# Attention beside projections: score tiles in groups of three steps up to step 236

## The chip, the cores and the metric

The kernel runs on one core of a Trainium2 chip. The core has a matrix engine (TensorE; PE in the profile, with PEld for its weight loads), a vector engine (VectorE, DVE), an activation engine (ScalarE, ACT), GpSimd (POOL) and a queue engine (SyncE, SP) that issues transfers. What is measured is the device time of one execution in microseconds (us); less is better. The time before is the median of three runs.

## The reference

The program is a stack of four sublayers on a sequence of 2048 rows with 640 columns: attention, Fourier mixing, attention, Fourier mixing, all with the same weights. Each works on a layer norm of its input and is added to it.

```python
def _A_ref(x, wqkv, wo):            # H = 32 heads, Dh = 20
    qkv = (x @ wqkv).reshape(B, S, 3, H, Dh) ...
    scores = jnp.einsum("bhqd,bhkd->bhqk", q, k) * (Dh ** -0.5)
    p = _softmax(scores, axis=-1)
    o = jnp.einsum("bhqk,bhkd->bhqd", p, v)
    return o.transpose(0, 2, 1, 3).reshape(B, S, D) @ wo
...
x = x + _A_ref(_layernorm(x), A_wqkv, A_wo)
x = x + _B_ref(_layernorm(x), ...)  # Real(DFT_seq(DFT_hidden(x)))
x = x + _A_ref(_layernorm(x), A_wqkv, A_wo)
x = x + _B_ref(_layernorm(x), ...)
```

Everything is computed in 32-bit floats. Projections are made as three products of split operands (high times high, high times low, low times high), so that they are exact enough.

## The kernel before

A layer has a prologue (layer norm, transposes, the first chunks of q and k, half of v), the attention, the output projection and the Fourier part. The change is in the attention.

**Steps.** Attention is a list of 512 steps in each layer (`Attention.steps`): eight groups `g` of four heads, four blocks `qb` of 512 queries, sixteen blocks `kc` of 128 keys. `scores(n, j)` makes one score tile of step n, for two heads: two matmuls of 62 rows, side by side in the array (rows 0 and 64), into one of three PSUM banks that go round, `p{(2n+j)%3}`, and then one exponential on ScalarE over 128 x 1024 elements into one of seven buffers `e`, which go round as well. A step has two score tiles. `values(n)` multiplies the four exponentials of a step with v and adds into one PSUM bank, `acc`; each of its four matmuls shows as two records in the profile. After the last key block, `finish` transposes that bank out on VectorE, normalizes, and stores on GpSimd's queue. In the profile the score matmuls are `psc`, the values `acc`, the exponentials `e<-psc`.

**Blocks.** The rest of q, k and v is projected during the attention. `Qkv.work()` gives it out in blocks of matmuls into one PSUM bank (`fill`): a product of 15 matmuls (five chunks, three passes) is cut by `pieces` into eight and seven, for a q or k chunk of 128 columns (`pqk`, 512 wide) and for v (`pv`, 320 wide). A q or k product is then split on VectorE and stored (`keep`), and two steps later a small matmul makes the norms of it (`pn`, `norms`). A v product is only copied out (`own`). `need` asks that a chunk be made before a group of heads begins to load it, and gives out blocks at once if it isn't.

**Sweep.** `sweep` sets the order by hand. For each step it calls `begin` (tasks, bounds, needs), issues the loads of q and k on SyncE's queue, makes the two score tiles, calls `fill` (which gives out at most one block, if `due` says that blocks are behind their marks), and then some values. Up to step `THIN` = 236, a step with a block makes no values (unless kc is 1), and the next step makes all that are owed, up to two steps behind the scores. After step 236 blocks are sparser and values follow under another rule, which stays. The marks before are 16 blocks by step 44 and 74 by step 236; 107 are all.

**Loads.** `qload` fetches the next block of q, with a bound for the exponent (`shiftb`), at kc 4 of the block before. For the groups in `LATE` (4 and 6 before) it goes at kc 10, with a bound made anew in each block (`bound`: kc 5, 8 and 10), so that their q chunk need be made only a block of 512 rows at a time.

**Other work.** `compare` gives VectorE a few tasks of a check that runs along (the tiles `cq`, `far`, `ctop`); ScalarE does hardly anything but exponentials in the attention.

Of the kernel before, what the change touches and what calls it, by code (L numbers as in the profile page):

```python
# [23 lines left out]
GUARD = 30.0  # L24
NP = NT // 2
NQ = NT // 4
LATE = (256 // (4 * DH) + 1, 512 // (4 * DH))
FIRST = (0, 1, 4, 5)
HD = D // 2
TOL = 2.0 ** -32  # L30
# [5 lines left out]
def mha_fnet_kernel(ctx, tc, x_in, wqk, wv, wo, seq, hid, nat_seq, nat_hid, out):  # L36
# [65 lines left out]
    def pieces(blocks, n):  # L102

        todo = [f for b in blocks for f in b]
        for i in range(0, len(todo), n):
            for f in todo[i:i + n]:
                f()
            yield i + n < len(todo)
# [23 lines left out]
    class Qkv:  # L132
# [248 lines left out]
        def work(s):  # L381

            order = [ND + 1, 1, ND + 2, 2, ND + 3, 3, ND + 4, 4]
            w = {0: s.w1}

            def chunk(i):
                c = order[i]
                for tb in range(NB):
                    p = bank("fill", [128, 512], "pqk")
                    for more in pieces([s.product(p, w[i], tb, dc) for dc in range(ND)], 8 if (i, tb) < (5, 1) else 5):  # L390
                        if more:
                            yield True
                    sq = s.keep(p, c, tb, True, s.fill)

                    def after():
                        s.norms(bank("fill", [H, 512], "pn"), c, tb, sq)
                        s.made.add((c, tb))
                        if tb == NB - 1:
                            s.made.add(c)
                            if i + 1 < len(order):  # L400
                                w[i + 1] = s.weights(s.fill("w", [2, ND, 128], F32R, "wqk"), order[i + 1], True)
                            if i + 2 < len(order):
                                s.fetch(order[i + 2])
                    yield after

            for i in range(4):
                yield from chunk(i)
            for t in range(NT):
                p = bank("fill", [128, HD], "pv")
                for more in pieces([s.value(p, t, dc) for dc in range(ND)], 8):  # L410
                    if more:
                        yield True
                s.own(p, t, 1, True)
                yield None
            s.made.add("v")
            for i in range(4, 8):
                yield from chunk(i)

            s.silent = True
            r = s.bounds()  # L420
            ok = const.tile([128, 1], F32, name="ok", bufs=2)
            V.tensor_scalar(ok[:H], r[:H, 2:3], (GUARD / SCALE) ** 2, None, op0=OP.is_le)

            def after():
                p = bank("fill", [1, 1], "pok")
                PE.matmul(p, ok[:H], one[:H], start=True, stop=True)
                V.tensor_scalar(s.flag, p, float(H), None, op0=OP.is_equal)
            yield after
# [25 lines left out]
    class Attention:  # L454
# [95 lines left out]
                    G.dma_start(s.o[k, h * DH:(h + 1) * DH, qb * 512:(qb + 1) * 512],  # L550
                                hl[k][32 * j:32 * j + DH])

        def sweep(s, shift, begin, fill):
            done = calm = 0
            for n, (g, qb, kc) in enumerate(s.steps):
                begin(n, g, qb, kc)
                last = qb == NB - 1
                if kc == (7 if last else 10 if g in LATE else 4) and not (last and g == H // 4 - 1):
                    s.qload(*((g, qb + 1) if not last else (g + 1, 0)), shift)
                if last and g + 1 < H // 4:  # L560
                    for f, j in {1: [(0, 0)], 9: [(0, 1)], 11: [(1, 0)]}.get(kc, []):
                        s.kload(g + 1, f, j)
                if qb == 0 and kc == 0 and g:
                    s.kload(g, 1, 1)
                s.scores(n, 0)
                s.scores(n, 1)

                more, owed = fill(n) and n >= 2 and n + 1 < len(s.steps), n - 1 - done  # L570
                if n < s.THIN:
                    if more and kc != 1:
                        continue
                    count = owed
                else:
                    if more and owed < 3:
                        calm = n + 2
                        continue
                    count = min(owed, 1)
                    if owed > 1 and (done + 1) % NT and n >= calm:  # L580
                        calm = n + 2
                        count = 2
                for _ in range(count):
                    s.values(done)
                    done += 1
            for n in range(done, len(s.steps)):
                s.values(n)

        def run(s, done, project, check):

            work, tasks, later = s.a.work(), s.a.vweights(1, s.a.fill, pause=[lambda: None] * 2), list(check)
            s.work, s.blocks, s.after, s.rest, s.more, s.landed = True, 0, None, 0, False, 0

            marks = ((0, 0), (44, 16), (s.THIN, 74))

            def due(n):
                for (n0, k0), (n1, k1) in zip(marks, marks[1:]):
                    if n < n1:
                        return s.blocks < k0 + (k1 - k0) * (n - n0) / (n1 - n0)
                return s.blocks < 74 or s.blocks >= 107 or (n - 1) % NT in (2, 7, 12)  # L600

            def block(n):
                try:
                    f = next(work)
                    s.blocks += 1
                    s.more = f is True
                    s.after = (n + (2 if n < s.THIN else 4), f) if f and not s.more else None
                    s.rest = s.after[0] + 2 if s.after else n
                except StopIteration:
                    s.work = False  # L610
                    tasks.extend(done())

            def fill(n):
                if s.after:
                    if n >= s.after[0]:
                        f, s.after = s.after[1], None
                        f()
                elif s.work and n >= s.rest and (s.more and n < s.THIN or due(n + 1)):
                    block(n)
                    s.rest = max(s.rest, n + 2)  # L620
                    return s.work and not s.a.silent

            def compare(n):


                if n < 8:
                    return
                for _ in range(2):
                    if not later or n < s.landed or (len(check) - len(later)) * 490 >= n * len(check):
                        break  # L630
                    task = later.pop(0)
                    if isinstance(task, tuple):
                        s.landed = n + 5
                        task = task[1]
                    task()

            def need(n, *keys):
                while not all(k in s.a.made for k in keys):
                    if s.after:
                        fill(s.after[0])  # L640
                    else:
                        block(n)

            def begin(n, g, qb, kc):


                if qb == NB - 1 and g + 1 < H // 4:
                    when, to = 0, g + 1
                    c0, c1 = to * 80 // 128, ((to + 1) * 80 - 1) // 128
                    keys = [c0, (c1, 0) if to in LATE else c1, ND + c0, ND + c1] + (["v"] if to >= 4 else [])  # L650
                else:
                    when, to, keys = 5, g, [(((g + 1) * 80 - 1) // 128, qb + 1)]
                if to != g or g in LATE and qb < NB - 1:
                    if kc == when:
                        need(n, *keys)
                        s.shift = s.a.bound(to, s.room)
                    if kc - when in (0, 3, 5):
                        next(s.shift)

                if tasks and n % 2 == 0 and n >= 16 and n % 64 < 54:  # L660
                    tasks.pop(0)()
                for f in project.early.get(n, []):
                    f()

            def between(n):
                more = fill(n)
                compare(n)
                return more

            s.sweep("b", begin, between)  # L670
            assert not s.work and not later and not tasks, (len(later), len(tasks))

        def general(s, done, project):
# [35 lines left out]
                for j in range(2):  # L709
                    s.kload(0, f_, j)  # L710
            s.qload(0, 0, "m")
            s.sweep("m", lambda *_: None, lambda *_: None)
            for f in sum(project.early.values(), []):
                f()

# [813 lines left out]
```

## Time and profile before

| | |
|---|---|
| median of the runs | 2512.77 us (2511.39 to 2512.98) |
| profiled execution | 2511.93 us, its span 2510.1 us |
| busy: PE / ACT / DVE / POOL | 2479.9 / 2133.1 / 980.2 / 524.1 us |
| score matmuls (L518) | 4096, 786.2 us |
| value matmul records (L529) | 8192, 1057.9 us |
| exponentials (L521) | 2048, 1934.4 us |
| attention, layer 0, first score to step 236 | 86.6 to 598.5 us |
| attention, layer 1, first score to step 236 | 1330.2 to 1842.4 us |

The profile is of one execution. Its time includes some 2 us outside of the span. A matmul's end is modelled, so busy time of PE is no measure of how much it could still do; what counts is the time from the start of one run of equal matmuls to the start of the next. A row of the timeline merges equal instructions that follow each other: start, length, engine, line, operation, tiles written and read, shapes, and how many (x). In brackets stands how long the engine had been idle and what released it.

### The profile page before, as it was taken

The numbers are of one execution on the slowest core, as the hardware profiler recorded it, in microseconds if no ns is written. First come the engines' busy times: TensorE is split into PE (matmuls) and PEld (weight loads), VectorE is DVE, ScalarE is ACT, GpSimd is POOL, SyncE is SP. The second block draws the span as 40 slices with busy tenths as digits, with TensorE's granted clock in tenths as the row PEclk, the third lists the DMA queues.
The fourth block names the chain that finished last, engine by engine and source line by source line (L and its number), as shares of the span: only waits on it lengthen the run. The fifth ranks groups of instructions, "written<-read, shape, count | busy, mean of one in ns | idle before, by whom it ended". The sixth has DMA issues, their size and how long they took to land. (4 is left out here: it accounts for less than half of the span.)

```text
span 2510.1 us, 43669 instructions
## 1 busy us (share of the span) xinstructions
PE 2479.9 (99%) x16350; PEld 1147.5 (46%) x16350; DVE 980.2 (39%) x2144; ACT 2133.1 (85%) x2430; POOL 524.1 (21%) x1028
## 2 busy tenths in 40 slices
PE   8999999999999999999999999999999999999998
PEld 7644434433333332249885444444433333322596
DVE  6245422234243333416753444223233333332275
ACT  6688899989999999985457888999899999999752
POOL 2012111111212212113321121111121122221233
PEclk9999999999999999999999999999999999999999
DMA  5224221223222224327553332212131322233355
GB/s 188 95 88 126 81 90 44 83 72 94 86 90 86 94 86 123 118 89 245 190 182 100 114 111 91 80 57 65 59 100 51 92 62 71 58 108 96 115 211 195
DMA packets 127241, 262.58 MB, mean 105 GB/s; under 512 B 28952, under 2 KB 53304, under 8 KB 127020
## 3 DMA queue, kind: packets, MB, share of 16 engines
q1 hardware_dynamic: 88428, 159.83, 19.7%
q0 software_dynamic: 38592, 99.85, 12.6%
q8 instruction: 132, 2.16, 0.4%
q14 instruction: 89, 0.73, 0.1%
HBM read 175.29 MB, written 84.26 MB: 103 GB/s over the span
## 5 line engine op out<-in xcount | busy, mean ns | idle before, releaser
L521 ACT ACTIVATE e<-psc 128x1024 f32<-128x1024 f32 x2048 | 1934.4, 1121 | 126.0 <-PE psc L518 94.1
L529 PE MATMUL acc<-e,v 128*32 128x512 f32 x8192 | 1057.9, 602 | 3.9 <-DVE of L536 3.8
L518 PE MATMUL psc<-stq,stk 62*128 62x512 f32 x4096 | 786.2, 455 | 1.3 <-ACT e L521 1.3
L518 PEld LDWEIGHTS psc<-stq,stk 62*128 62x128 f32 x4096 | 335.5, 184 | 792.3 <-ACT e L521 762.6
L529 PEld LDWEIGHTS acc<-e,v 128*32 128x32 f32 x8192 | 188.9, 108 | 381.6 <-issue 358.4
L99 PE MATMUL pqk<-xt,wqk 128*128 128x512 f32 x1200 | 319.6, 407 | 2.1 <-DVE top L213 1.4
L550 POOL DMA_DIRECT2D o<-oh x256 | 131.5, 522 | 872.5 <-DVE oh L545 871.4
L84 DVE CAST hl<-pqk 128x512 fp32r<-128x512 f32 x64 | 44.3, 692 | 553.5 <-PE pqk L99 553.5
L99 PEld LDWEIGHTS pqk<-xt,wqk 128*128 128x128 f32 x1200 | 213.2, 188 | 90.3 <-issue 43.5
L536 DVE STREAM_TRANSPOSE of<-acc 128x512 f32<-128x512 f32 x64 | 45.8, 716 | 349.9 <-PE acc L529 349.3
L99 PE MATMUL pv<-wv,xt 128*128 128x320 f32 x960 | 159.7, 316 | 0.0
L99 PEld LDWEIGHTS pv<-wv,xt 128*128 128x128 f32 x960 | 141.1, 188 | 24.7 <-issue 21.2
L550 POOL DMA_DIRECT2D o<-ot x256 | 128.5, 510 | 1.9 <-issue 1.4
L207 POOL DMA_DIRECT2D scrq<-hl x40 | 28.1, 704 | 446.1 <-DVE hl L87 311.4
L243 DVE COPY v<-pv 128x320 f32<-128x320 f32 x32 | 15.7, 491 | 235.3 <-PE pv L99 235.3
L765 DVE TENSOR_REDUCE far<-cq 128x1 f32<-128x512 f32 (+5 forms) x169 | 98.5, 584 | 5.7
L92 PE MATMUL py<-wo,o 128*128 128x320 f32 x320 | 99.1, 310 | 1.4 <-DVE xr L947 1.4
L207 POOL DMA_DIRECT2D scrk<-hl x40 | 28.0, 699 | 344.3 <-DVE hl L87 300.2
L93 PE MATMUL py<-wo,o 128*128 128x320 f32 x320 | 98.6, 308 | 0.0
L94 PE MATMUL py<-wo,o 128*128 128x320 f32 x320 | 98.6, 308 | 0.0
L769 DVE TENSOR_TENSOR cq<-cq 128x512 f32<-128x512 f32 (+4 forms) x166 | 96.4, 580 | 2.4 <-DMA cq<-in_nat_seq_dram 2.4
L213 DVE TENSOR_REDUCE top<-pn 32x1 f32<-32x512 f32 x80 | 53.5, 676 | 107.4 <-PE pn L212 107.4
(200 smaller groups left out, 1729.2 us busy)
## 6 DMA issues: line engine op xcount, KB each, us to landing
cq<-in_nat_seq_dram POOLq DMA_DIRECT2D x64, 512.0 KB, 5.3
scrq<-hl POOLq DMA_DIRECT2D x40, 512.0 KB, 3.2
scrk<-hl POOLq DMA_DIRECT2D x40, 512.0 KB, 3.2
stq<-scrq SPq DMA_DIRECT2D x256, 80.0 KB
stk<-scrk SPq DMA_DIRECT2D x128, 160.0 KB
o<-o SPq DMA_DIRECT2D x16, 1280.0 KB
stq<-scrq SPq DMA_DIRECT2D x256, 40.0 KB
stk<-scrk SPq DMA_DIRECT2D x128, 80.0 KB
```

The source lines that it names most:

```text
L92: PE.matmul(out_ap, ah, bh, start=start, stop=False)
L93: PE.matmul(out_ap, ah, bl, start=False, stop=False)
L94: PE.matmul(out_ap, al, bh, start=False, stop=stop)
L99: yield lambda i=i, j=j, k=k: PE.matmul(out_ap, a[i], b[j], start=dc == 0 and k == 0, stop=dc == ND - 1 and k == 2)
L207: G.dma_start(s.scr["qk"[k]][c * 128:(c + 1) * 128, :, tb * 512:(tb + 1) * 512], hl.bitcast(F32))
L213: V.tensor_reduce(s.top[:H, c // ND, c % ND, tb:tb + 1], p, op=OP.max, axis=AX.X)
L518: PE.matmul(p[:, i], s.k[g, kc // 8, j][r, kc % 8 * 128:(kc % 8 + 1) * 128], s.q[g, qb, j][r], start=True, stop=True)
L521: A.activation(e, p, AF.Exp, scale=SCALE)
L529: PE.matmul(s.acc[32 * j:32 * j + 32], s.a.v[kc][:, v0:v0 + 32], s.e[n, j // 2][:, j % 2], start=kc == 0, stop=kc == NT - 1, skip_group_ch ...
L550: G.dma_start(s.o[k, h * DH:(h + 1) * DH, qb * 512:(qb + 1) * 512], hl[k][32 * j:32 * j + DH])
L765: V.tensor_reduce(to, x, op=OP.max, axis=AX.X, apply_absolute_value=True)
L769: V.tensor_tensor(y, x, y, op=op)
```

## The change

Up to step 236, where a block is due (`plan`), three steps are now taken together: three score tiles, the block, three score tiles, and then the values of three steps, from the one before the group on. Groups begin at key blocks 1 to 14 only. A step outside of a group makes its two score tiles and all values that are owed, now up to one step behind. Blocks up to step 236 come only in groups. A v product is no longer cut (a piece of 15), so 91 blocks are all, and the mark is 58 blocks by step 236, at an even pace from the start. Group 1 joins `LATE`: its q chunk (the second) need be made only block by block. The tasks on VectorE (`compare`) follow the scores instead of the block. The rest of the diff passes these functions into `sweep` and counts n one later, without effect on the order after step 236.

```diff
-LATE = (256 // (4 * DH) + 1, 512 // (4 * DH))
+LATE = (1, 4, 6)
...
-                for more in pieces([s.value(p, t, dc) for dc in range(ND)], 8):
+                for more in pieces([s.value(p, t, dc) for dc in range(ND)], 15):
...
-        def sweep(s, shift, begin, fill):
-            done = calm = 0
-            for n, (g, qb, kc) in enumerate(s.steps):
+        def sweep(s, shift, begin, fill=lambda n: None, plan=None, compare=lambda n: None):
+            done = calm = n = 0
+
+            def opened(n):
+                g, qb, kc = s.steps[n]
                 begin(n, g, qb, kc)
...
+            while n < len(s.steps):
+                opened(n)
+                piece = plan and plan(n)
+                if piece:
+
+                    for t in range(2 * n, 2 * n + 6):
+                        if t > 2 * n and t % 2 == 0:
+                            opened(t // 2)
+                        s.scores(*divmod(t, 2))
+                        if t == 2 * n + 2:
+                            piece()
+                        if t % 2:
+                            compare(t // 2)
+                    n += 3
+                    while done < n - 1:
+                        s.values(done)
+                        done += 1
+                    continue
                 s.scores(n, 0)
                 s.scores(n, 1)
                 more, owed = fill(n) and n >= 2 and n + 1 < len(s.steps), n - 1 - done
-                if n < s.THIN:
-                    if more and kc != 1:
-                        continue
-                    count = owed
+                compare(n)
+                n += 1
+                if plan and n <= s.THIN:
+                    count = owed + 1
+                elif more and owed < 3:
+                    calm = n + 1
+                    continue
                 else:
-                    if more and owed < 3:
-                        calm = n + 2
-                        continue
...
-            marks = ((0, 0), (44, 16), (s.THIN, 74))
+            marks = ((0, 0), (s.THIN, 58))
...
-                return s.blocks < 74 or s.blocks >= 107 or (n - 1) % NT in (2, 7, 12)
+                return s.blocks < 58 or s.blocks >= 91 or (n - 1) % NT in (2, 7, 12)
...
-                elif s.work and n >= s.rest and (s.more and n < s.THIN or due(n + 1)):
+                elif s.work and n >= max(s.rest, s.THIN) and due(n + 1):
...
+            def plan(n):
+                if n % NT in range(1, NT - 1) and n + 3 <= s.THIN and not s.after and n >= s.rest and (s.more or due(n + 1)):
+                    return lambda: block(n + 1)
...
-            s.sweep("b", begin, between)
+            s.sweep("b", begin, fill, plan, compare)
```

More of the change, by code (lines that the diff above doesn't have):

```diff
@@ L570, in sweep @@
                 more, owed = fill(n) and n >= 2 and n + 1 < len(s.steps), n - 1 - done
-                if n < s.THIN:
-                    if more and kc != 1:
-                        continue
-                    count = owed
-                else:
-                    if more and owed < 3:
-                        calm = n + 2
-                        continue
+                compare(n)
[5 more added lines that the diff above has]
+                    continue
+                else:
                     count = min(owed, 1)
-                    if owed > 1 and (done + 1) % NT and n >= calm:
-                        calm = n + 2
+                    if owed > 1 and (done + 1) % NT and n > calm:
+                        calm = n + 1
                         count = 2
@@ L663, in begin @@
                     f()
[L665 to L668, printed above, removed]
-            s.sweep("b", begin, between)
+            s.sweep("b", begin, fill, plan, compare)
             assert not s.work and not later and not tasks, (len(later), len(tasks))
@@ L711, in general @@
             s.qload(0, 0, "m")
-            s.sweep("m", lambda *_: None, lambda *_: None)
+            s.sweep("m", lambda *_: None)
             for f in sum(project.early.values(), []):
```

## The prediction

> **What bounds the kernel now.** I read the busy time by stage first, then TensorE's timeline inside one stage, then ScalarE's. In each layer I cut the attention at the first score matmul of step 236, which is found by counting four score matmuls per step.
>
> ```profile
> 86.60:598.50 511.90, 508.82 (x3395) 210.34 (x3394) 185.94 (x376) 453.52 (x473) 89.56 (x158) 1.00 0.28 87
> 598.50:1118.40 519.90, 519.68 (x3511) 172.42 (x3507) 181.52 (x397) 514.01 (x554) 99.35 (x179) 1.00 0.30 92
> 1330.20:1842.40 512.20, 508.56 (x3395) 210.22 (x3394) 183.12 (x360) 453.80 (x473) 89.37 (x159) 1.00 0.28 86
> ```
>
> Columns: stretch, length, then busy time of PE, weight loads, DVE, ACT, POOL, and the clock (1.00). After step 236 ACT is busy 514.0 of 519.9 us with its exponentials, whose number stays, so nothing here can move that stretch. Up to step 236 (511.9 us in layer 0, 512.2 in layer 1) ACT has 58 us to spare and PE is full. The change lives there, twice. One unit of projection work in that stretch looks like this on PE:
>
> ```profile
> 210.36 2.14 PE L99 MATMUL pqk<-xt,wqk 128*128 128x512 f32 x8
> 212.43 0.73 PE L518 MATMUL psc<-stq,stk 62*128 62x512 f32 x4
> 213.09 1.92 PE L529 MATMUL acc<-e,v 128*32 128x512 f32 x16
> 214.94 0.73 PE L518 MATMUL psc<-stq,stk 62*128 62x512 f32 x4
> 215.61 1.91 PE L99 MATMUL pqk<-xt,wqk 128*128 128x512 f32 x7
> 217.44 0.73 PE L518 MATMUL psc<-stq,stk 62*128 62x512 f32 x4
> 218.10 1.92 PE L529 MATMUL acc<-e,v 128*32 128x512 f32 x16
> 219.96 0.73 PE L518 MATMUL psc<-stq,stk 62*128 62x512 f32 x4
> 220.63 1.24 PE L529 MATMUL acc<-e,v 128*32 128x512 f32 x8
> 221.80 0.73 PE L518 MATMUL psc<-stq,stk 62*128 62x512 f32 x4
> 222.46 1.07 PE L529 MATMUL acc<-e,v 128*32 128x512 f32 x8
> 223.46 0.73 PE L518 MATMUL psc<-stq,stk 62*128 62x512 f32 x4
> 224.12 0.50 PE L99 MATMUL pqk<-xt,wqk 128*128 128x512 f32 x1
> ```
>
> Durations are modelled, so I price a run from its start to the next run's start. Scores of a step: 0.66. Values of one step (8 records): 1.00; of two (16): 1.85, so a step more is 0.86 and each run of values has a fixed 0.14. Projection pieces: 2.07 for eight matmuls, 1.83 for seven, 0.24 per matmul. A lone step is 221.80 to 223.46, 1.66; one with the norms matmul (pn) is 1.84 (219.96 to 221.80). ACT has gaps here, so PE's switches cost time.
>
> **The change on PE alone.** Three score tiles in a row need one price that the steady part lacks. It stands at the start of layer 0, where PE (and PEld, its weight loads) shows:
>
> ```profile
> 89.35 0.98 PE L518 MATMUL psc<-stq,stk 62*128 62x512 f32 x6
> 89.93 0.40 PE L518 MATMUL psc<-stq,stk 62*128 62x512 f32 x2
> 90.97 0.19 PEld L518 LDWEIGHTS psc<-stq,stk 62*128 62x128 f32 x2 [1.09 <-ACT e L521]
> 90.97 0.50 PE L518 MATMUL psc<-stq,stk 62*128 62x512 f32 x2 [0.65 <-ACT e L521]
> 91.40 0.50 PE L99 MATMUL pqk<-xt,wqk 128*128 128x512 f32 x1
> ```
>
> The x6 row is 0.98 long where an x4 row is 0.73, so a third pair costs about 0.24: three tiles take 0.90, and the third starts 0.58 after the first (89.35 to 89.93). A pair that had to wait (90.97) takes 0.43 until the next run; an unhindered last pair takes 0.90 - 0.58 = 0.32. A wait in mid-run costs 0.11 on top, its weight load not having been made before.
>
> A projection unit now takes 6 steps; in the new order of the instructions it takes 8: group with eight matmuls, group with seven, a lone step with pn, a lone step.
> - Before, 8 steps: 224.12 - 210.36 = 13.76, plus two lone steps 3.32: 17.08.
> - After: (0.90 + 2.07 + 0.90 + 2.71) + (0.90 + 1.83 + 0.90 + 2.71) + 1.84 + 1.66 = 16.42, with three steps of values at 1.85 + 0.86 = 2.71.
> - Saved: 0.66, the two runs of scores and two of values that are gone.
>
> A unit of v (320 columns):
>
> ```profile
> 320.44 0.87 PE L518 MATMUL psc<-stq,stk 62*128 62x512 f32 x4
> 321.23 1.43 PE L99 MATMUL pv<-wv,xt 128*128 128x320 f32 x8
> 322.60 0.73 PE L518 MATMUL psc<-stq,stk 62*128 62x512 f32 x4
> 323.26 1.92 PE L529 MATMUL acc<-e,v 128*32 128x512 f32 x16
> 325.12 0.73 PE L518 MATMUL psc<-stq,stk 62*128 62x512 f32 x4
> 325.78 1.29 PE L99 MATMUL pv<-wv,xt 128*128 128x320 f32 x7
> 327.00 0.73 PE L518 MATMUL psc<-stq,stk 62*128 62x512 f32 x4
> 327.67 0.64 PE L529 MATMUL acc<-e,v 128*32 128x512 f32 x4
> ```
>
> Before, 4 steps: scores 4 x 0.66, pieces 1.37 + 1.22, values 2 x 1.86: 8.95, and a wait of 0.13 in the first run (0.79, not 0.66). After: one piece of 15, 1.37 + 7 x 0.15 = 2.42; the group 0.90 + 2.42 + 0.90 + 2.71 = 6.93, and a lone step: 8.59. Saved: 0.36.
>
> The order has 21 projection units and 16 of v in the 236 steps of a layer: 21 x 0.66 + 16 x 0.36 = **19.6 us saved** if nothing waits.
>
> **The waits that come in.** Score tiles go round three banks, so tile t waits for the exponential of tile t-3; a third tile in a row therefore waits for the last exponential of the step before the group. ACT's pace:
>
> ```profile
> 226.19 0.73 PE L518 MATMUL psc<-stq,stk 62*128 62x512 f32 x4
> 226.79 1.02 ACT L521 ACTIVATE e<-psc 128x1024 f32<-128x1024 f32 x1 [0.62 <-PE psc L518]
> 316.06 6.53 ACT L521 ACTIVATE e<-psc 128x1024 f32<-128x1024 f32 x7 [0.28 <-PE psc L518]
> 89.90 1.94 ACT L521 ACTIVATE e<-psc 128x1024 f32<-128x1024 f32 x2 [0.77 <-PE psc L518]
> ```
>
> An idle ACT starts 0.60 after the run of scores does, ends 1.02 later, and each further one ends 0.92 after the last ((6.53 - 1.02) / 6). The bank is free 0.05 after that (89.90 + 1.02 = 90.92, the pair starts at 90.97). The 2.71 of values ahead of the lone steps lets ACT run dry, so I start its chain there.
> - Projection unit, first group: chain from the pn step's start: exponentials end at 1.62, 2.54, 3.46, 4.38, bank free at 4.43. PE is at its third tile at 1.84 + 1.66 + 0.58 = 4.08. Wait 0.35 (0.09 of it in the second lone step's values, which now follow one step behind the scores and not two), plus 0.11: 0.46. After its piece, at the group's last tile: the bank is free at 4.38 + 3 x 0.92 + 0.05 = 7.19, PE is there at 4.43 + 0.43 + 2.07 + 0.58 = 7.51: none.
> - Second group: ACT starts dry. After the piece of seven, PE is there at 0.90 + 1.83 + 0.58 = 3.31, the bank free at 1.62 + 2 x 0.92 + 0.05 = 3.51: 0.20 + 0.11 = 0.31.
> - Unit of v, one lone step ahead: free at 2.59, PE there at 1.66 + 0.58 = 2.24: 0.35 + 0.11 = 0.46. After the long piece: free at 2.54 + 3 x 0.92 + 0.05 = 5.35, PE there at 2.59 + 0.43 + 2.42 + 0.58 = 6.02, none.
>
> Per layer 21 x 0.77 + 16 x 0.46 = **23.5 us added**: the saving is eaten.
>
> **Waits that go.** The 0.13 of each v unit: 2.1. The hand-over of the accumulator, when values of a new q block follow the last ones with only one step's scores between:
>
> ```profile
> 506.28 0.73 PE L518 MATMUL psc<-stq,stk 62*128 62x512 f32 x4
> 507.19 0.64 PE L529 MATMUL acc<-e,v 128*32 128x512 f32 x4 [0.18 <-DVE of L536]
> ```
>
> That is 0.91 for 0.66. The order has this pattern 8 times in a layer's first 236 steps, afterwards 4 times: 1.0 less.
>
> **The other edits.** Group 1 joins LATE: three more bounds in each layer (five small DVE instructions, one on POOL, one DMA on SP each), and q loads that go out late. A late load in the profile, on SP's queue:
>
> ```profile
> 954.06 0.79 SPq L496 DMA_DIRECT2D stq<-scrq  x1
> ...
> 961.90 0.25 SPq L499 DMA_DIRECT2D stq<-shiftb  x1
> 969.33 0.98 PE L518 MATMUL psc<-stq,stk 62*128 62x512 f32 x4
> ```
>
> Twelve DMAs were issued in 8.1 us, 7.2 us ahead of the first score that reads them, at ACT's pace; group 1's steps are slower, so the margin is no smaller. I cost it at nothing, covered by that margin; if it failed, six loads (three per layer) would be paid in PE time. Moved on SP and POOL are weight fetches and k and q stores; between one piece and the next lie at least 3 steps. The extra bounds delay DVE by under 1 us each, between a piece and its pn, which now lie 0.90 + 2.71 + 0.66 = 4.3 us apart (before 0.66 + 1.85 + 0.66 = 3.2). The larger v piece fills the same single bank, emptied long before the next. All at nothing; bounds -0.5 to +1.5 per layer.
>
> **Sum.** Per layer -19.6 + 23.5 - 2.1 - 1.0 = +0.8; two layers +1.6. The profiled execution took 2511.93 us (span 2510.1), so 2513.5; the median of the runs, 2512.77, lies 0.84 above it: **2514.4**. About 0.2%, 5 us, is what a measurement can tell from no change. Uncertain are the 58 waits (0.05 each, 2.9 per layer) and the 116 third tiles (0.02 each, 2.3 per layer): own range 2506 to 2522.
>
> The Trainium skill, "TensorE: Matmul & The Clock Gate", section "Back-to-back issue gap", gives N/2.4 + 2.5 ns, 216 ns for 512 columns; the rows have 0.24 us per matmul in mixed work. By the page 116 x 0.024 = 2.8 us per layer would come off, 2508.8 as an estimate; I go by the rows.
>
> **Rivals.**
> - *Slower: ACT paces.* The exponentials end 0.97 apart instead of 0.92 while PE works in longer runs. Each of 58 waits follows about three spacings: 58 x 3 x 0.05 = 8.7 per layer, 2514.4 + 17.4 = 2532. It decides from 0.02 more (7 us). For: the pace was read beside runs of at most four score matmuls and 16 value records, not six and 24. Against: it held 0.92 over six spacings with PE at full work. The Trainium skill, "Perfetto Trace Analysis", section "Optimization Strategy", says that a repeated gap on the engine that should be full can mean too little PSUM for the next tile; the wait at 90.97 is such a gap, and no run here shows the new order.
> - *Faster: no reload.* The weight load of a waiting tile is made ahead, and the 42 + 16 = 58 waits cost 0.11 less: 6.4 per layer, 2501.6. Against: the weight load itself stands at 90.97, waiting for ACT. The Trainium skill, "TensorE: Matmul & The Clock Gate", section "What happens when you issue a matmul", says that TensorE pulls weight loads ahead of running matmuls; in that row it did not.
> - *Faster: ACT has caught up.* No new waits: 2511.93 - 2 x 22.7 + 0.84 = 2467. The wait at 90.97 speaks against it.
> - *q late.* Each of six loads 5 us late: 2544. The 7.2 us margin is against it.
> - *The groups don't form.* Excluded: the order shows all 58 pieces with six score matmuls on either side or ten.
>
> **Chances.** Forecast, within 0.2%: 0.52. ACT paces: 0.25; q late: 0.04; together slower 0.29. No reload: 0.11; caught up, in part or whole: 0.08; together faster 0.19. The range reaches into both sides: 2501 to 2526.
>
> **What would show it.** Runs of six score matmuls at 0.90 where nothing waits and near 1.3 before a piece (after lone steps); runs of 24 value records at 2.71; PE waiting for e on some 58 tiles per layer before step 236, ACT still short of full there; step 236 reached about 0.8 us later in each layer; the rest unchanged. A third tile at 0.30, or exponentials spaced 0.97, would make the time longer; waits under 0.2 would make it shorter.

## The result, and the profile after

The changed kernel takes 2515.45 us (median of 20 runs, 2514.93 to 2518.22) against 2511.66 for the kernel before (20 runs): a ratio of 1.0016, 95% interval 1.0009 to 1.0022. That is 3.8 us slower, small but beyond the noise, and inside the 0.2% that the prediction called no change; 2514.4 had been forecast. In the profiled executions the span grew by 2.9 us (2510.1 to 2513.0), and the time outside of it from 1.8 to 2.6; the latter was not forecast, and what makes it was not settled.

The stretches of the changed kernel, cut at step 236 of each layer as before (length, then busy PE, weight loads, DVE, ACT, POOL, clock):

```profile
86.60:600.70 514.10, 504.25 (x3402) 219.42 (x3401) 187.55 (x390) 444.26 (x473) 90.47 (x161) 1.00 0.27 85
600.70:1120.40 519.70, 519.29 (x3504) 172.18 (x3501) 182.21 (x398) 513.11 (x552) 99.63 (x180) 1.00 0.30 93
1332.20:1845.50 513.30, 504.10 (x3402) 219.29 (x3401) 183.99 (x369) 443.83 (x473) 90.78 (x161) 1.00 0.28 86
```

Up to step 236 they are 2.2 and 1.1 us longer (511.9 and 512.2 before); the stretch after step 236 is 0.1 to 0.2 shorter, the same but for noise. The small difference up to step 236 hides two large terms of opposite sign, which one projection unit on PE shows:

```profile
252.79 1.29 PE L518 MATMUL psc<-stq,stk 62*128 62x512 f32 x6
254.01 2.78 PE L529 MATMUL acc<-e,v 128*32 128x512 f32 x24
256.72 0.73 PE L518 MATMUL psc<-stq,stk 62*128 62x512 f32 x4
257.40 1.24 PE L529 MATMUL acc<-e,v 128*32 128x512 f32 x8
258.57 0.74 PE L518 MATMUL psc<-stq,stk 62*128 62x512 f32 x4
259.23 1.16 PE L529 MATMUL acc<-e,v 128*32 128x512 f32 x8
260.33 1.37 PE L518 MATMUL psc<-stq,stk 62*128 62x512 f32 x6
261.62 2.11 PE L99 MATMUL pqk<-xt,wqk 128*128 128x512 f32 x8
263.67 0.96 PE L518 MATMUL psc<-stq,stk 62*128 62x512 f32 x6
264.56 2.78 PE L529 MATMUL acc<-e,v 128*32 128x512 f32 x24
267.27 0.96 PE L518 MATMUL psc<-stq,stk 62*128 62x512 f32 x6
268.16 1.88 PE L99 MATMUL pqk<-xt,wqk 128*128 128x512 f32 x7
```

The runs are what the rows of before had priced: 24 value records 2.71 (254.01 to 256.72), six score matmuls 0.89 where nothing waits (263.67 to 264.56). The waits stand where they were put: 1.29 instead of 0.89 after two lone steps (260.33 to 261.62), with 0.10 in the second lone step's values (1.10, not 1.00); 1.22 after a piece of seven (252.79 to 254.01); none after the piece of eight. ScalarE's rows beside it:

```profile
250.68 5.61 ACT L521 ACTIVATE e<-psc 128x1024 f32<-128x1024 f32 x6 [0.76 <-PE psc L518]
257.35 6.54 ACT L521 ACTIVATE e<-psc 128x1024 f32<-128x1024 f32 x7 [1.07 <-PE psc L518]
264.26 2.86 ACT L521 ACTIVATE e<-psc 128x1024 f32<-128x1024 f32 x3 [0.37 <-PE psc L518]
```

It is idle for 1.07 us, from late in the run of 24 values until 0.63 after the start of the lone step's scores (256.72 to 257.35), and then ends one exponential every 0.92 us: ((6.54 - 1.02) / 6). If the prediction's chain of arrivals is right, that idle time is what PE waits for later; the experiments test it.

### The profile page after: what moved, and what is told of

It reads as the page before. It is cut to its first block, busy times and chain, and to the rows that moved or that the text cites. A ratio compares the mean times of both kernels' runs of the same rounds, so it can differ in the third digit from the quotient of the medians.

```text
span 2513.0 us, 43736 instructions
## 1 busy us (share of the span) xinstructions
PE 2470.3 (98%) x16350; PEld 1165.4 (46%) x16350; DVE 985.0 (39%) x2174; ACT 2112.0 (84%) x2430; POOL 526.5 (21%) x1034
## 3 DMA queue, kind: packets, MB, share of 16 engines
q1 hardware_dynamic: 88644, 159.88, 19.6%
## 5 line engine op out<-in xcount | busy, mean ns | idle before, releaser
L521 ACT ACTIVATE e<-psc 128x1024 f32<-128x1024 f32 x2048 | 1913.4, 1120 | 149.9 <-PE psc L518 139.4
L529 PE MATMUL acc<-e,v 128*32 128x512 f32 x8192 | 1045.1, 601 | 3.8 <-DVE of L536 3.7
L529 PEld LDWEIGHTS acc<-e,v 128*32 128x32 f32 x8192 | 203.0, 108 | 399.4 <-issue 375.8
L99 PE MATMUL pv<-wv,xt 128*128 128x320 f32 x960 | 151.3, 313 | 0.0
```

The costliest lines, as they stand in the source:

```text
L99: yield lambda i=i, j=j, k=k: PE.matmul(out_ap, a[i], b[j], start=dc == 0 and k == 0, stop=dc == ND - 1 and k == 2)
L521: A.activation(e, p, AF.Exp, scale=SCALE)
L529: PE.matmul(s.acc[32 * j:32 * j + 32], s.a.v[kc][:, v0:v0 + 32], s.e[n, j // 2][:, j % 2], start=kc == 0, stop=kc == NT - 1, skip_group_ch ...
```

## The experiments

The theory: up to step 236 TensorE's own runs set the time; the change saves some 20 us per layer of run ends and loses as much in waits for exponentials, because a third score tile in a row needs the bank of the step before. Rivals: longer runs cost more by themselves; another edit of the change costs the time; the waits are somewhere else. Ratios are to the kernel before, which was measured again beside each set of runs (2512.01, then 2512.07).

**Half of the exponentials left out**, in both kernels:

```diff
-            A.activation(e, p, AF.Exp, scale=SCALE)
+            A.activation(e[:, 0], p[:, 0], AF.Exp, scale=SCALE) if n < s.THIN else A.activation(e, p, AF.Exp, scale=SCALE)
...
-                PE.matmul(s.acc[32 * j:32 * j + 32], s.a.v[kc][:, v0:v0 + 32], s.e[n, j // 2][:, j % 2],
+                PE.matmul(s.acc[32 * j:32 * j + 32], s.a.v[kc][:, v0:v0 + 32], s.e[n, j // 2][:, j % 2 if n >= s.THIN else 0],
```

> The kernel before, with the exponentials of steps before 236 made over one of the two heads of a score tile only (512 of 1024 columns); the values of the other head are multiplied with the same half, so half of the exponentials of that stretch is left out and all matmuls stay. Theory (the time up to step 236 is TensorE's own runs plus waits for exponentials): the kernel before hardly waits for them there, so 2 to 4 us less than before, about 2508.5. Rival (ScalarE paces that stretch in the kernel before as well): tens of us less.

> The changed kernel with the same half of the exponentials left out before step 236. Theory: the waits of third score tiles go and what TensorE saves by fewer runs is left, some 20 us per layer under the shortened kernel before: about 2469, 39 us under it. Rival A (a third tile or a run of 24 value records costs more by itself than the rows said, and that ate the saving): no faster than the shortened kernel before, within 5 us. Rival B (the v blocks or the later q loads cost the time): 20 to 35 us under it at most, and still PE waits that are not for exponentials.

Measured: the shortened kernel before 2508.94 us, ratio 0.9987 (0.9977 to 0.9996) to the kernel before; the shortened changed kernel 2465.12, ratio 0.9814 (0.9797 to 0.983). With short exponentials the change is worth 43.8 us. Layer 0 up to step 236, first the shortened kernel before, then the shortened changed kernel:

```profile
86.80:596.60 509.80, 507.15 (x3393) 208.06 (x3392) 185.93 (x376) 264.30 (x473) 89.81 (x158) 1.00 0.28 87
```

```profile
86.70:575.40 488.70, 486.63 (x3400) 217.17 (x3399) 187.55 (x390) 256.66 (x473) 89.98 (x161) 1.00 0.29 89
```

509.8 - 488.7 = 21.1 us is what the change saves on TensorE when the exponentials are short. 514.1 - 488.7 = 25.4 us is what the exponentials take back in the changed kernel; in the kernel before they take 511.9 - 509.8 = 2.1. And -21.1 + 25.4 - 2.1 = +2.2, which is the layer's loss. (In layer 1 the three are 21.9, 24.6 and 1.6.) Added up over the trace of layer 0, about 23 of the 25.4 us lie in runs of scores that wait, and 2.6 in values of lone steps; the pieces and the runs of 24 values are as long in both. The run after lone steps that had been 1.29 long is bare in the shortened changed kernel (251.59 to 252.48):

```profile
250.59 1.06 PE L529 MATMUL acc<-e,v 128*32 128x512 f32 x8
251.59 0.96 PE L518 MATMUL psc<-stq,stk 62*128 62x512 f32 x6
252.48 2.09 PE L99 MATMUL pqk<-xt,wqk 128*128 128x512 f32 x8
```

So longer runs cost nothing by themselves, and ScalarE did not pace the stretch up to step 236 in the kernel before.

**Values placed otherwise in the changed kernel.** No run is saved, values only move between runs:

```diff
                     n += 3
-                    while done < n - 1:
+                    left = 0 if plan(n) or (n - 2) % NT == NT - 1 else 1
+                    while done < n - 1 - left:
...
                 if plan and n <= s.THIN:
                     count = owed + 1
+                    if count == 1 or n % NT != 1 and not plan(n):
+                        count = min(count, 1)
```

> The changed kernel with the values placed otherwise: a group that a lone step follows makes two steps of values and not three, lone steps stay two behind, and the lone step ahead of a group makes two steps of values. The runs are as many as in the changed kernel. Theory: TensorE now comes to a group's third score tile 0.86 later and finds its bank free (3.10 against 2.59 in a v unit), and ScalarE doesn't run dry in a run of 24: most of the 37 waits ahead of pieces and some of those after go, 14 to 17 us per layer, 2481 to 2488. Rival (the time was lost in switching, not in waiting for exponentials): 2515 within 3, since no run is saved.

Measured: 2485.93 us, ratio 0.9898 (0.9882 to 0.9915) to the kernel before, 29.5 under the changed kernel. That is faster than both kernels, and the waits are what went. A unit of it on PE:

```profile
255.28 1.92 PE L529 MATMUL acc<-e,v 128*32 128x512 f32 x16
257.13 0.97 PE L518 MATMUL psc<-stq,stk 62*128 62x512 f32 x6
258.03 2.11 PE L99 MATMUL pqk<-xt,wqk 128*128 128x512 f32 x8
...
266.49 1.30 PE L518 MATMUL psc<-stq,stk 62*128 62x512 f32 x6
267.72 1.92 PE L529 MATMUL acc<-e,v 128*32 128x512 f32 x16
```

Two steps of values ahead of the group let its three score tiles through unhindered (0.90, 257.13 to 258.03). The wait after the piece of seven stays (1.23, 266.49 to 267.72). Over the whole of layer 0 the waits ahead of pieces fall from 14.7 us to about 1, those after pieces of seven stay at 7, and those after pieces of eight grow from nothing to 3; the stretch is 500.0 us long where it was 514.1. The time was lost in waiting, then, not in switching.

**The cut into seven and eight**, alone in the changed kernel, as a control in the kernel before, and with the values placed otherwise:

```diff
-        for i in range(0, len(todo), n):
-            for f in todo[i:i + n]:
+        cuts = [0, 7, len(todo)] if n == 8 else [*range(0, len(todo), n), len(todo)]
+        for i, k in zip(cuts, cuts[1:]):
+            for f in todo[i:k]:
                 f()
-            yield i + n < len(todo)
+            yield k < len(todo)
```

> The changed kernel with each product of 15 matmuls cut into seven and eight, not eight and seven. Theory: the group after two lone steps has a backlog on ScalarE that covers a piece of seven (7.19 against 7.27), and in the second group the piece of eight puts the last score tile at 3.55, after its bank is free (3.51): 21 waits of 0.31 per layer go, 13 us in all, 2502.5. Rival (the cut doesn't matter, since the same matmuls run): 2515.5 within 2.

> Control for the cut into seven and eight, in the kernel before. Theory: no third tiles stand in a row there, so the order of the cuts changes no wait for exponentials: 2512 within 1.5. Rival (seven before eight is better by itself, through VectorE's work after the product): as much faster as in the changed kernel, 2505.

> The changed kernel with the values placed as in spread2 and the products cut into seven and eight. Theory: in spread2 ScalarE has a backlog when the first group begins; a piece of seven there brings TensorE to the last tile 0.24 earlier, so the waits move from the second group to the first and little is left to gain: 2485 within 2. Rival (the two savings add): 2479.

Measured: 2508.24 us in the changed kernel, ratio 0.9986 (0.9976 to 0.9995) to the kernel before; 2510.99 as a control, 0.9995 (0.9986 to 1.0005), no difference; 2485.65 with both, 0.9896 (0.988 to 0.9913), the same as without the cut: a piece of seven is still followed by a wait (a run of about 1.22), now in the first group. The changed kernel gained 7.2 us, not 13. Its second group shows why, on PE and PEld (one line was added, so the scores are L519):

```profile
251.67 0.30 PEld L519 LDWEIGHTS psc<-stq,stk 62*128 62x128 f32 x4 [0.36 <-ACT e L522]
251.67 1.08 PE L519 MATMUL psc<-stq,stk 62*128 62x512 f32 x6
252.24 0.19 PEld L519 LDWEIGHTS psc<-stq,stk 62*128 62x128 f32 x2 [0.28 <-ACT e L522]
252.67 2.78 PE L530 MATMUL acc<-e,v 128*32 128x512 f32 x24
...
279.07 1.18 PE L519 MATMUL psc<-stq,stk 62*128 62x512 f32 x6
280.18 2.78 PE L530 MATMUL acc<-e,v 128*32 128x512 f32 x24
```

The third pair's weights are loaded at 252.24, 0.57 after the run's start: PE is hardly late, the wait itself is gone, but the run takes 1.00 and not 0.89. The bank came free after the point at which the load would have been made ahead, and the 0.11 of the late load stays. So it is in 39 of the 42 second groups of the two layers (0.98 to 1.01), 2.1 us in layer 0. The first groups, which now have the piece of seven, lose another 1.4 there, 1.0 of it in four real waits like the one at 279.07 (1.11), which the expectation had ruled out. In the unhindered run of the changed kernel all six loads stand in one row, 0.53 long, ahead of their matmuls:

```profile
263.66 0.53 PEld L518 LDWEIGHTS psc<-stq,stk 62*128 62x128 f32 x6 [0.35 <-issue]
```

**Parts of the change alone, in the kernel before.** The v products whole, with the marks to match:

```diff
-                for more in pieces([s.value(p, t, dc) for dc in range(ND)], 8):
+                for more in pieces([s.value(p, t, dc) for dc in range(ND)], 15):
...
-            marks = ((0, 0), (44, 16), (s.THIN, 74))
+            marks = ((0, 0), (44, 16), (s.THIN, 58))
...
-                return s.blocks < 74 or s.blocks >= 107 or (n - 1) % NT in (2, 7, 12)
+                return s.blocks < 58 or s.blocks >= 91 or (n - 1) % NT in (2, 7, 12)
```

> The kernel before with one part of the change alone: v products whole (a piece of 15), with the marks moved to match (16 blocks by step 44, 58 by step 236). Theory: 16 piece starts fewer per layer save 16 x 0.17 = 2.7, but 16 pieces fewer also merge 16 runs of values fewer (16 x 0.14 = 2.2), and the longer piece moves work past the accumulator's hand-overs; so no gain from this part, 2511 to 2518. Rival (the whole v products are what the change gains by): 2506 or less.

Measured: 2519.84 us, ratio 1.0031 (1.002 to 1.0043), 1.8 us beyond the slow end of what was expected. More lone steps follow each other, and there the scores wait for ScalarE (0.84, 323.70 to 324.54), and one hand-over of the accumulator waits 0.80:

```profile
323.70 0.91 PE L518 MATMUL psc<-stq,stk 62*128 62x512 f32 x4
324.54 1.07 PE L529 MATMUL acc<-e,v 128*32 128x512 f32 x8
...
340.99 1.07 PE L529 MATMUL acc<-e,v 128*32 128x512 f32 x8 [0.80 <-DVE of L536]
```

Up to step 236 the profiled layers are 2.2 and 2.0 us longer; the span is 7.8 longer. The other 3.6 us lie before the attention and after step 236, and what makes them was not settled. Whole v products are no gain without the groups; what they do inside of the groups no run shows alone.

The late q of group 1:

```diff
-LATE = (256 // (4 * DH) + 1, 512 // (4 * DH))
+LATE = (1, 4, 6)
```

> The kernel before with one part alone: group 1 loads its q late, with a bound made anew in each block (LATE = 1, 4, 6). Theory: hidden; six small VectorE instructions per block beside a full TensorE, 2512 within 1.5. Rival (q late): scores wait for their loads or the accumulator's hand-over waits for VectorE, 2514 or more.

Measured: 2512.44 us, ratio 1.0002 (0.9992 to 1.0011): hidden. In the changed kernel a load of group 1 was issued from 310.70 to 317.46 on SP's queue (the rows show issuing, not landing), and the first score that reads it came at 327.28, 9.8 us later:

```profile
310.70 0.80 SPq L496 DMA_DIRECT2D stq<-scrq  x1
...
317.22 0.24 SPq L499 DMA_DIRECT2D stq<-shiftb  x1
```

## Why the prediction was right

The mechanism was right: what fewer runs save, waits for a third bank take back. That the sum came out so near owes something to luck, because terms were off in both directions.

- *The bound.* Right: the stretch after step 236 kept its length, and the span grew before it. The 0.8 us more outside of the span are no part of it.
- *The saving.* 20.6 per layer were forecast, 19.6 for the runs and 1.0 for the hand-overs; 21.1 were measured with short exponentials in layer 0. The parts agree less well. The runs gave some 21: the third tile came out at 0.89 and not 0.90, the whole v piece at 2.40 and not 2.42, and two places per layer where a projection block had waited 0.43 for VectorE are gone, which was not forecast. The hand-overs did not become cheaper. In the kernel before, five runs per layer are 0.25 too long for this reason (not eight); in the changed kernel three are, and one waits 1.21, because VectorE prepares weights (`wqk`) before it takes the accumulator out:

```profile
363.71 0.73 PE L518 MATMUL psc<-stq,stk 62*128 62x512 f32 x4
364.07 0.83 DVE L87 TENSOR_TENSOR wqk<-wraw,wqk 128x640 fp32r<-128x640 f32 x1
364.81 0.71 DVE L536 STREAM_TRANSPOSE of<-acc 128x512 f32<-128x512 f32 x1
365.58 1.07 PE L529 MATMUL acc<-e,v 128*32 128x512 f32 x8 [1.14 <-DVE of L536]
```

That is 0.7 more where 1.0 less stood in the sum.
- *The waits that come in.* 23.5 forecast, 25.4 measured in layer 0: this term was a little small, and no kind of wait is off by more than 0.7. The single waits agree: 0.10 + 0.40 after two lone steps (forecast 0.46 together), 0.42 on average ahead of a v piece (0.46), 0.33 after the piece of seven (0.31), none after the piece of eight. The arithmetic counted a wait only where PE arrives before the bank is free; the cut into seven and eight shows that a late load is paid without it.
- *The waits that go.* 2.1 per layer were forecast, all of it in the v units, and the kernel before loses 2.1 in layer 0 to exponentials. This agreement is luck: the first runs of the 16 v units wait 0.08 on average, 1.3 in all, since the row that the forecast read (0.13) is above the mean. The rest lies in the first group of steps of the layer (0.4) and elsewhere.
- *Other edits.* Nothing, as forecast for q; its margin was 9.8 us in the row shown. The moved weight work, put at nothing as well, is what the long hand-over above waits for.
- *The sum.* +0.8 per layer forecast; +2.2 and +1.1 up to step 236 measured. Against the kernel before that is +3.8 us where +1.6 stood. The level, 2514.4 against 2515.45, is nearer than the difference, because the kernel before came out at 2511.66 over 20 runs and not at the 2512.77 of the first three. The result lies inside the likeliest case's own range.
- *The rivals.* ScalarE's pace stayed at 0.92, so it did not slow the longer runs down. The reload is paid at each wait, as the load's row in the trace of before said. The time at which ScalarE has caught up (2467 forecast) exists: the shortened changed kernel reached 2465.12, though with half of the exponentials left out.

The Trainium skill, "Perfetto Trace Analysis", section "Optimization Strategy", says that a gap which repeats on the engine that should be full can mean too little PSUM for the next tile. Here it fits: the gap of 0.40 ahead of a piece is a third tile waiting for one of three banks. Whether a fourth bank would close it no run shows; moving one step of values, 0.86 us, ahead of the group closed nearly all the gaps ahead of pieces without one.

## What to carry to other kernels

Here fewer, longer runs on the full engine (TensorE) paid only as far as the engine that frees its banks (ScalarE) was kept in work. So count, for each tile, when its bank comes free and when the full engine arrives there, over a whole cycle and not as an average. Where a long run of one kind lets the other engine run dry, try dividing it so that work lies just ahead of the place that waits; here that was worth 29.5 us. An average share of busy time (ScalarE had 58 us to spare in that stretch) says nothing about such waits. And price a wait by the mean over all its places, not by the one row at hand: two terms of this forecast agree in the sum and not in the rows.

## What was not expected of the hardware

A score tile whose bank comes free shortly before TensorE arrives costs 0.11 us although its matmul hardly waits: its weight load stood at 252.24, beside its matmul and not ahead of it, and the run took 1.00 us where an unhindered one takes 0.89. In the cut into seven and eight this is paid in 39 of 42 second groups, and it is the larger part of what that cut fell short by (7.2 us for 13).
